# Four attention layers in turn, sliding and full: operand loads two quads ahead, layer norm by token tile, output weights in one load, and squares formed as they fall due

## The chip, the cores and the metric

The kernel runs on one core of one Trainium2 chip. The metric is the device time of one execution in microseconds (us), taken as the median of several runs. A core has a TensorE (PE) for matrix products, a VectorE (DVE), a ScalarE (ACT) and a GpSimd (POOL) for the rest, and a SyncE (SP), whose only work in this kernel is to issue DMA transfers, one after the other, from one queue.

## The reference

One sequence of S = 2048 tokens, width D = 512, H = 32 heads of Dh = 16, float32. Two kinds of attention alternate, each on the layer norm of the running sum. The A layers see a window of the last 256 tokens, the B layers all tokens, with no causal mask.

```python
def _A_ref(x, wqkv, wo):                       # layers 0 and 2
    qkv = (x @ wqkv).reshape(B, S, 3, H, Dh)   # transposed to q, k, v of (B, H, S, Dh)
    scores = jnp.einsum("bhqd,bhkd->bhqk", q, k) * (Dh ** -0.5)
    mask = (idx[:, None] - idx[None, :] >= 0) & (idx[:, None] - idx[None, :] < W)   # W = 256
    scores = jnp.where(mask[None, None], scores, -1e9)
    o = jnp.einsum("bhqk,bhkd->bhqd", _softmax(scores), v)
    return o.transpose(0, 2, 1, 3).reshape(B, S, D) @ wo

# _B_ref (layers 1 and 3): the same without the mask

x = A_x
x = x + _A_ref(_layernorm(x), A_wqkv, A_wo)
x = x + _B_ref(_layernorm(x), B_wqkv, B_wo)
x = x + _A_ref(_layernorm(x), A_wqkv, A_wo)
x = x + _B_ref(_layernorm(x), B_wqkv, B_wo)
```

## The kernel before

**Tiling.** The 2048 queries are four chunks c of 512, the 32 heads eight quads of four. A sliding layer goes through the chunks, in each through the eight quads, in each through three score steps; a step forms scores of two pairs of heads on PE (`s<-qt,kt`, L760), takes the exponential of each pair on ACT (`e<-s`, L764), cuts the window's edges on POOL (L832, L835) and adds to the sums with PE (L842). A full layer has sixteen steps a quad, each with two exponentials of 128 x 1024 (scores L756, sums L809). Layer 3 is cut once more by the four groups t of eight heads, so it has sixteen units (t, c) of two quads.

**Operands.** Products are kept exact by splitting numbers in two float16 parts. Queries and keys lie in DRAM as rows of such parts (`qs`, `kw` for sliding layers, `kf` for full ones). `load_win` (L786) and `load_full` (L773) bring the `qt` and `kt` of a quad; there are two `qt` buffers and three `kt` buffers, and `attention` (L1016) issues the loads of a quad one quad ahead. Weights are loaded raw (`load_w`, L314, tiles `wr`), split by ACT and DVE (`split`, L326) and stored to DRAM (`wd`); each use loads a megabyte from there. The raw and split weights use the four `vf` buffers, which in the full layers hold the values. The output weights (s = 3) are loaded as eight pieces of 16 partitions, since their rows have to lie in another order. Weights in use sit in two rings: ring 0 (`w`, two slots) and ring 1 (`vw`, three slots).

**Side work.** Between the score steps stand the projections of the next chunk or layer (`keys`, `queries`, `values`), the output product `wo` with the residual sum, and the layer norm of what comes out (`norm`). Each is a generator in a `Work`; a `Side` spreads a chunk's works over its steps, opens their weights ahead (`prefetch`, `may_open`), and `finish` runs what is left at the end of a chunk or unit. Between two layers lies a tail, in which the last chunk's output, norm and first projections run with no attention beside them.

**What sets the order.** PE's order, and in the full layers DVE's too, is the order in which this code issues it, by a clock of planned times (`clock[0]`): a work that waits gives a time before which it isn't taken up. On all other engines and in SP's queue a scheduler sets the order from priorities and its own estimates. Each engine, and SP's queue, then runs strictly in its order.

**Squares.** Softmax needs bounds: for every chunk the largest sum of squares of a key (`km`, L569) and each query's own (`m`, L595) are formed from the projected `sp` by POOL or DVE (`sq`), PE (`b<-sq,hsum`, L550, L553) and DVE. `keys` and `queries` put that on the list `pend` with a due time, 3.6 planned us later (4.6 in full layers), and `settle` does what is due. The keys of layers 1 and 3 share one maximum per head group over all chunks, and `key_shift` stores what follows from it; in layer 3 a work of its own, `shift3`, settles everything on the list and calls it.

**Layer norm.** `norm` has its passes over the four 128-token tiles of a chunk (three each, L449 and L455) issued by `turns` (L252), in sliding layers all at once; the transposes through the DMA (L477) follow.

A path for inputs outside of the bounds stands behind the kernel and does not run here.

Of the kernel before, what the change touches and what calls it, by code (L numbers as in the profile page):

```python
# [19 lines left out]
P = 128  # L20
# [170 lines left out]
def fast_path(ctx, tc, flag, a_x, a_wqkv, a_wo, b_wqkv, b_wo, out):  # L191
# [76 lines left out]
    ident = cp.tile([P, P], F32, name="ident")  # L268
# [45 lines left out]
    def load_w(ty, s):  # L314
        raw = wp.tile([P, NC, D], F32, name=f"wr{ty}_{s}", tag="vf", bufs=NQ)
        if s < 3:
            nc.sync.dma_start(raw, mats[ty, s].rearrange("(k p) f -> p k f", p=P))
        else:

            for u in range(2):  # L320
                for h in range(4):
                    nc.sync.dma_start(raw[32 * h + DH * u:32 * h + DH * u + DH],
                                      mats[ty, s].rearrange("(k u h d) f -> u h d k f", u=2, h=4, d=DH)[u, h])
        return raw

    def split(ty, s, raw):  # L326

        w = wp.tile([P, NC, 2, D], F16, name=f"w{ty}_{s}", tag="vf", bufs=NQ)
        for k in range(NC):
            nc.scalar.activation(w[:, k, 0], raw[:, k], AF.Copy, scale=WS)  # L330
            nc.vector.scalar_tensor_tensor(w[:, k, 1], raw[:, k], WS, w[:, k, 0], op0=ALU.mult, op1=ALU.subtract)
            yield
        nc.sync.dma_start(wd[ty, s], w)
        return w
# [150 lines left out]
    def project(l, s, c, act, ht=None):  # L485
# [3 lines left out]
        w = weights(ty, s, n, *((0, D, 0) if ht is None else (ht * P, (ht + 1) * P, l == 3 and not act)))  # L489
# [70 lines left out]
    def keys(l, c, act, ht=None, then=None):  # L560
        sqs = yield from project(l, 1, c, act, ht)
# [10 lines left out]
        pend.append((clock[0] + (4.6 if PH["full"] else 3.6), rest))  # L572

    def queries(l, c, act, ht=None):
        sqs = yield from project(l, 0, c, act, ht)
# [22 lines left out]
        pend.append((clock[0] + (4.6 if PH["full"] else 3.6), rest))  # L598
# [30 lines left out]
    def early_queries(l):  # L629

        PRE["q"] = pp.tile([P, 2, QC], F16, name=f"qt{l}_0_0", tag="qt", bufs=2)
# [39 lines left out]
    def wo(l, c, tail):  # L671
# [4 lines left out]
        for i in range(4):  # L676
# [9 lines left out]
            if i == 3 and not PH["full"]:  # L686
                yield from norm(l + 1, c, xs, tail)
# [22 lines left out]
    def epilogue(l, c, qd, a):  # L710
# [14 lines left out]
        def scaled():  # L725
            den = ot[:, :, DH]
            nc.vector.tensor_tensor(lmin, lmin, den, ALU.min)
            nc.vector.tensor_add(lsum, lsum, den)
# [5 lines left out]
            nc.vector.tensor_tensor(OT[t][:, :, u, :], ot[:, :, :DH], r[:, :, None].broadcast_to([P, QC // 32, DH]), ALU.mult)  # L734

# [37 lines left out]
    def load_full(l, c, qd):  # L773
# [12 lines left out]
    def load_win(l, c, qd):  # L786
        n = f"{l}_{c}_{qd}"
        kt = pp.tile([P, 2, S // 2], F16, name=f"kt{n}", tag="kt", bufs=3)
        qt = pp.tile([P, 2, QC], F16, name=f"qt{n}", tag="qt", bufs=2)
# [60 lines left out]
    class Work:  # L850
# [25 lines left out]
        def may_open(self):  # L876
# [7 lines left out]
        done = begun = open = going = False  # L884
# [4 lines left out]
        def advance(self):  # L889
# [18 lines left out]
            elif isinstance(c, tuple):  # L908
                self.ready = c[1]
                return 0.0  # L910
            return c

    class Side:
# [65 lines left out]
        def share(self):  # L979
# [3 lines left out]
            if pend and not PH["busy"] and clock[0] >= max(PH["free"], pend[0][0]):  # L983
# [32 lines left out]
    def attention(l, works):  # L1016
# [5 lines left out]
        for t in range(NHT if l == 3 else 1):  # L1022
            for c in range(NQ):
# [9 lines left out]
                ops = load(l, c, qds[0])  # L1033
                for qd in qds:
# [8 lines left out]
                    nxt = load(l, c, qd + 1) if qd + 1 in qds else None  # L1043
# [25 lines left out]
                    ops = nxt  # L1069
# [18 lines left out]
    def K3(c, ht, act=False):  # L1088
        return Work(later(keys, 3, c, act, ht, key_shift if c == NQ - 1 and ht == 0 else None), PK / 4, ("K3", c, ht), [("T", 3, c)], True, ring=not act)

    def Q3(c, ht, act=False, after=()):
        return Work(later(queries, 3, c, act, ht), PK / 4, ("Q3", c, ht), [("T", 3, c), *after], True, ring=not act)

    def K1(ht, act=False):
        return Work(later(keys, 1, NQ - 1, act, ht, key_shift), PK / 4, ("K1", ht), [("T", 1, NQ - 1), ("P", 1, 1)], True)

    def shift3(ht):
        def gen():
            settle()
            key_shift(3, ht)  # L1100
            yield -1e-6
        return Work(gen(), 0.0, ("S3", ht), [("K3", c, ht) for c in range(NQ)])
# [68 lines left out]
    run(vals)  # L1171
    all_of([NN(1), T(0, 1)])
# [45 lines left out]
    def side3(t, c):  # L1218
        a = [last_lower(3)] if (t, c) == (0, 0) else []
        a += [Q3(c + 1, t)] if c < 3 else []  # L1220
        if t < 3:
            a.append(K3(c, t + 1))
            if c == 3:
                a += [shift3(t + 1), Q3(0, t + 1)]
        if t < 2 and (t or c > 1):
            a.append(upper(3, 2 * t + c // 2, range(2 * (c % 2), 2 * (c % 2) + 2)))
        if (t, c) != (0, 0):
# [7 lines left out]
             2: [VV(3, 0, True, (0,)), OO(2, 3, True), VV(3, 1, True, (0,), late(3)), VV(3, 2, True, (0,), late(3)), VV(3, 0, True, (1,), late(3)), T(3, 3), K3(3, 0, True)]}  # L1235
# [54 lines left out]
```

## Time and profile before

| what | value |
|---|---|
| median of 3 runs | 2723.62 us (2723.14 to 2728.02) |
| profiled execution, its own time | 2721.88 us |
| its span | 2720.2 us |
| mean granted clock of TensorE | 0.988 |
| PE / ACT / DVE / POOL busy, share of the span | 91% / 87% / 41% / 19% |
| DMA | 360.80 MB in 341159 packets, 117800 of them under 512 B |
| start | 0 to 50 us |
| layer 0 (sliding), then its tail | 50 to 426, to 474 us |
| layer 1 (full) | 474 to 1430 us |
| layer 2 (sliding), then its tail | 1430 to 1703, to 1746 us |
| layer 3 (full), end | 1746 to 2703, to 2720 us |

The profile is of one execution. A row of a timeline has the start, the duration, the engine, the line of the code, the operation, out<-in with sizes, the count, and in brackets the idle time ahead of it on its engine with what ended it. SPq is SP's queue of DMA issues; a row there has the time of issuing, not of landing. A row of waits has the engine, its line and what it waited for, then the total in us, the number of times and the longest.

### The profile page before, as it was taken

What the parts mean: (1) busy time and instruction counts of PE and PEld (TensorE: products, weight loads), DVE (VectorE), ACT (ScalarE), POOL (GpSimd) and SP (SyncE); (2) the same over time, 40 slices, a digit from 0 to 9 for tenths busy, and PEclk for the clock granted to TensorE, in tenths of its full rate; (3) what the DMA queues carried; (4) which work ended last, traced back from release to release, by engine and by line L of the source; (5) the groups of instructions that cost most, each with busy time, mean ns of one, the idle gap of its engine ahead of it and who ended that gap; (6) DMA issues with size and microseconds to landing.
All of it is one profiled execution on the core that took longest, in us unless ns stands there. A gap on an engine that the chain in (4) does not pass through costs nothing.

```text
span 2720.2 us, 113346 instructions
## 1 busy us (share of the span) xinstructions
PE 2487.6 (91%) x51023; PEld 1095.7 (40%) x51023; DVE 1110.8 (41%) x2342; ACT 2363.1 (87%) x2671; POOL 526.7 (19%) x1080
## 2 busy tenths in 40 slices
PE   7888999999998999999998999899999999988997
PEld 3233444444443444444443333544444444433332
DVE  5574554223434334334326666323333323333333
ACT  4575664999999999999995777499999999999996
POOL 1455551001100100100105778000000000000000
PEclk9999999999999999999999999999999999999999
DMA  8888865222324225333426565623233333334332
GB/s 283 233 253 248 241 193 162 82 90 86 108 91 126 92 90 138 94 100 102 110 71 192 160 194 148 167 72 117 81 107 100 96 96 105 109 106 123 122 118 98
DMA packets 341159, 360.80 MB, mean 133 GB/s; under 512 B 117800, under 2 KB 256568, under 8 KB 334392
## 3 DMA queue, kind: packets, MB, share of 16 engines
q1 hardware_dynamic: 340664, 353.46, 43.7%
q8 instruction: 401, 6.57, 1.0%
q14 instruction: 94, 0.77, 0.1%
HBM read 240.65 MB, written 96.99 MB: 124 GB/s over the span
## 4 chain that ended last, share of the span: by engine, by line
ACT 55%; PE 23%; issue 11%; DVE 7%; DMA 3%; POOL 1%; SPq 0%; ACTq 0%; DVEq 0%; POOLq 0%
ACT e L764 55%; PE b L403 9%; PE acc L842 4%; PE s L760 2%; PE acc L809 2%; PE s L756 2%; PE bs L403 1%; PE b L400 1%; DVE xh L455 1%; DVE xh L449 1%; DMA kt<-kw 1%; DVE xn L449 0%; DVE ot L723 0%; DMA wr<-in_A_wo_dram 0%; DMA wv<-wd 0%
## 5 line engine op out<-in xcount | busy, mean ns | idle before, releaser
L764 ACT ACTIVATE e<-s 128x1024 f32<-128x1024 f32 (+2 forms) x2432 | 2240.7, 1056 | 149.9 <-PE s L760 101.0
L809 PE MATMUL acc<-e,vt 64*17 64x512 f32 x16384 | 1085.6, 590 | 1.0 <-issue 1.0
L756 PE MATMUL s<-qt,kt 64*32 64x512 f16 x16384 | 850.8, 381 | 121.4 <-ACT e L764 99.8
L756 PEld LDWEIGHTS <-kt 64*32 64x32 f16 x16384 | 407.0, 89 | 931.3 <-issue 852.0
L809 PEld LDWEIGHTS acc<-e,vt 64*17 64x17 f32 x16384 | 281.0, 92 | 61.8 <-issue 3.8
L835 POOL TENSOR_SCALAR_AFFINE_SELECT e<-e 128x256 f32<-128x256 f32 x512 | 224.9, 445 | 189.7 <-ACT e L764 188.5
L832 POOL TENSOR_SCALAR_AFFINE_SELECT e<-e 128x256 f32<-128x256 f32 x448 | 199.2, 450 | 94.4 <-ACT e L764 91.9
L842 PE MATMUL acc<-e,vt 128*17 128x384 f32 (+2 forms) x2816 | 201.8, 394 | 6.4 <-POOL e L832 6.2
L741 POOL TENSOR_TENSOR oh<-o,oh 128x512 f16<-128x512 f32 x31 | 36.1, 1163 | 702.0 <-DVE oh L740 676.0
L403 PE MATMUL b<-xc,w 128*128 128x512 f16 x660 | 161.7, 392 | 9.8 <-DVE km L569 5.5
L706 DVE SCALAR_TENSOR_TENSOR x<-b,x 128x512 f32<-128x512 f32 x122 | 83.9, 688 | 193.1 <-PE b L400 189.8
L760 PE MATMUL s<-qt,kt 64*128 64x384 f16 (+2 forms) x1408 | 121.3, 279 | 43.7 <-ACT e L764 20.4
L422 DVE TENSOR_SCALAR sa<-acc 128x512 f32<-128x512 f32 x64 | 44.2, 691 | 281.4 <-PE acc L809 281.4
L528 POOL TENSOR_TENSOR sq_h<-sp_h 128x512 bf16<-128x512 f16 x29 | 42.9, 1479 | 546.4 <-DVE sp_h L522 537.6
L528 POOL TENSOR_TENSOR sq<-sp 128x512 bf16<-128x512 f16 x32 | 46.2, 1443 | 519.7 <-DVE sp L522 475.2
L400 PE MATMUL b<-xc,w 64*32 64x512 f16 x3072 | 126.5, 376 | 2.7 <-DVE j L423 1.5
L400 PE MATMUL b<-xc,w_h 64*32 64x512 f16 x2784 | 111.0, 376 | 3.9 <-DVE km L569 3.9
L400 PE MATMUL b<-wo,oh 64*32 64x512 f16 x2592 | 109.1, 376 | 5.4 <-DVE x L706 3.0
L403 PEld LDWEIGHTS <-w 128*128 128x128 f16 x720 | 67.0, 100 | 116.3 <-issue 46.4
L422 DVE TENSOR_SCALAR vt<-b 128x256 f32<-128x256 f32 (+1 forms) x36 | 18.4, 512 | 232.9 <-PE b L400 232.9
L760 PEld LDWEIGHTS <-kt 64*128 64x128 f16 x1408 | 52.0, 95 | 140.9 <-issue 114.8
L422 DVE TENSOR_SCALAR j_h<-b 128x512 f32<-128x512 f32 x29 | 20.0, 689 | 206.6 <-PE b L400 206.6
(134 smaller groups left out, 1905.9 us busy)
## 6 DMA issues: line engine op xcount, KB each, us to landing
kt<-kf SPq DMA_DIRECT2D x128, 512.0 KB
qt<-qs SPq DMA_DIRECT2D x128, 256.0 KB
xd<-x SPq DMA_DIRECT2D x96, 256.0 KB
x<-xd SPq DMA_DIRECT2D x96, 256.0 KB
w<-wd SPq DMA_DIRECT2D x21, 1024.0 KB
kt<-kw SPq DMA_DIRECT2D x64, 256.0 KB
qs<-sp SPq DMA_DIRECT2D x48, 256.0 KB
wo<-wd SPq DMA_DIRECT2D x12, 1024.0 KB
```

The costliest lines, as they stand in the source:

```text
L400: nc.tensor.matmul(ps[g:g + 32, r], a[k, g:g + 32], b[k], start=(i == 0), stop=(i == len(pairs) - 1), skip_group_check=True)
L403: nc.tensor.matmul(ps, a, b, start=(i == 0), stop=(i == len(pairs) - 1))
L422: nc.vector.tensor_scalar(dst, ps[0], scale, None, op0=ALU.mult)
L528: nc.gpsimd.tensor_tensor(sq, sp[:, 0], sp[:, 0], ALU.mult)
L706: nc.vector.scalar_tensor_tensor(xs[i], p, 1 / WS, xs[i], op0=ALU.mult, op1=ALU.add)
L756: nc.tensor.matmul(ps[g:g + 32, h], kt[R * h:R * h + R, pr, kc + g:kc + g + 32], qt[R * h:R * h + R, pr], start=True, stop=True, skip_grou ...
L760: nc.tensor.matmul(ps[:, h, s0:s0 + wd_], kt[R * h:R * h + R, pr, kc:kc + P], qt[R * h:R * h + R, pr, qc:qc + wd_], start=True, stop=True)
L764: nc.scalar.activation(e[:, :, w0:w1], ps[:, :, w0:w1], AF.Exp, scale=SCALE)
L809: nc.tensor.matmul(acc[r][32 * h:32 * h + DH + 1, :], V[l, qd // 4, j // 8][k, j % 8, 4 * (qd % 4) + h, :], es_[h // 2][k, h % 2, :], star ...
L832: nc.gpsimd.affine_select(v, v, pattern=[[0, 2], [-1, P]], compare_op=ALU.is_gt, fill=0.0, base=0, channel_multiplier=1)
L835: nc.gpsimd.affine_select(v, v, pattern=[[0, 2], [1, P]], compare_op=ALU.is_ge, fill=0.0, base=0, channel_multiplier=-1)
L842: nc.tensor.matmul(a[32 * h:32 * h + DH + 1, q * P:(q + nb) * P], V[l, (4 * c + j) // 4][:, j % 4, 4 * qd + h, :], es_[h // 2][:, h % 2, s ...
```

## The change

Lines of the changed kernel are shifted by up to five from those of before.

- Sliding layers keep two quads' operands loaded ahead (`ahead`, with a third `qt` buffer), and the first quad of layer 0 is loaded at the end of the start.
- `turns` waits, in sliding layers, between an operation of the layer norm and the next, so that the passes of one token tile are issued at a time.
- The output weights come in one load of 128 partitions; their eight pieces are now made in the store to `wd`.
- A work `wo` declares its weights' slot free after its last product (`freed`), ahead of the norm that follows in it. In the tails ring 1 may be opened, and the key projections there use it.
- Squares are due after 1.2 planned us in the tails. `share` also waits for the planned DVE, `finish` also waits for what is under way while squares are pending. `shift3` is gone: `key_shift` is called with the last chunk's keys when their squares fall due.
- The memset of the sliding layers' values goes from POOL to DVE, and three small things change place (`lmin` and `lsum` in the epilogue, and the buffer of `ident`).

```diff
@@ turns (L252)
-        for us, f in ops:
+        for i, (us, f) in enumerate(ops):
             soon(chain, us, lambda f=f: one(f))
+            if PH["win"] and i < len(ops) - 1:
+                yield wait(us + 0.7)
@@ load_w (L314)
-        if s < 3:
-            nc.sync.dma_start(raw, mats[ty, s].rearrange("(k p) f -> p k f", p=P))
-        else:
-            for u in range(2):
-                for h in range(4):
-                    nc.sync.dma_start(raw[32 * h + DH * u:32 * h + DH * u + DH],
-                                      mats[ty, s].rearrange("(k u h d) f -> u h d k f", u=2, h=4, d=DH)[u, h])
+        nc.sync.dma_start(raw, mats[ty, s].rearrange("(k p) f -> p k f", p=P))
@@ split (L326)
-        nc.sync.dma_start(wd[ty, s], w)
+        if s < 3:
+            nc.sync.dma_start(wd[ty, s], w)
+        else:
+            for u in range(2):
+                for h in range(4):
+                    r, p = 32 * h + DH * u, P // 2 * u + DH * h
+                    nc.sync.dma_start(wd[ty, s][r:r + DH], w[p:p + DH])
@@ keys, queries
-    def keys(l, c, act, ht=None, then=None):
-        sqs = yield from project(l, 1, c, act, ht)
+    def keys(l, c, act, ht=None, then=None, ring=0):
+        sqs = yield from project(l, 1, c, act, ht, ring)
...
-        pend.append((clock[0] + (4.6 if PH["full"] else 3.6), rest))
+        pend.append((clock[0] + (4.6 if PH["full"] else 3.6 if PH["win"] else 1.2), rest))
@@ values (L651)
-            nc.gpsimd.memset(vt[:, :, :, DH:], 1.0)
+            nc.vector.memset(vt[:, :, :, DH:], 1.0)
@@ wo
             if i == 3 and not PH["full"]:
+                if not tail:
+                    yield "freed", clock[0]
                 yield from norm(l + 1, c, xs, tail)
@@ load_full, load_win, early_queries
-        qt = pp.tile([P, 2, QC], F16, name=f"qt{n}", tag="qt", bufs=2)
+        qt = pp.tile([P, 2, QC], F16, name=f"qt{n}", tag="qt", bufs=3)
@@ Work.may_open
-                    (len(wused[self.ring]) < RINGS[self.ring] or wused[self.ring][-RINGS[self.ring]].done) and (PH["full"] or not self.ring)
+                    (len(wused[self.ring]) < RINGS[self.ring] or wused[self.ring][-RINGS[self.ring]].done or wused[self.ring][-RINGS[self.ring]].freed) and not (PH["win"] and self.ring)
@@ Side.share, Side.finish
-            if pend and not PH["busy"] and clock[0] >= max(PH["free"], pend[0][0]):
+            if pend and not PH["busy"] and clock[0] >= max(PH["free"], pend[0][0], vt_[0] - 0.2):
...
-            while any(not stays(w) for w in self.q):
+            while any(not stays(w) for w in self.q) or PH["busy"] and pend:
@@ attention
-                ops = load(l, c, qds[0])
+                ahead = deque([PRE.pop("w", None) or load(l, c, qds[0])])
+                if win:
+                    ahead.append(load(l, c, 1))
...
-                    nxt = load(l, c, qd + 1) if qd + 1 in qds else None
+                    ops = ahead.popleft()
+                    if qd + 1 + win in qds:
+                        ahead.append(load(l, c, qd + 1 + win))
@@ K3, K1, side3, start, tails
-        return Work(later(keys, 3, c, act, ht, key_shift if c == NQ - 1 and ht == 0 else None), PK / 4, ("K3", c, ht), [("T", 3, c)], True, ring=not act)
+        ring = not act if ring is None else ring
+        return Work(later(keys, 3, c, act, ht, key_shift if c == NQ - 1 else None, ring), PK / 4, ("K3", c, ht), [("T", 3, c)], True, ring=ring)
...
-        return Work(later(keys, 1, NQ - 1, act, ht, key_shift), PK / 4, ("K1", ht), [("T", 1, NQ - 1), ("P", 1, 1)], True)
+        return Work(later(keys, 1, NQ - 1, act, ht, key_shift, act), PK / 4, ("K1", ht), [("T", 1, NQ - 1), ("P", 1, 1)], True, ring=act)
...
-    def shift3(ht):
-        def gen():
-            settle()
-            key_shift(3, ht)
...
+    PRE["w"] = load_win(0, 0, 0)
     all_of([NN(1), T(0, 1)])
...
-                a += [shift3(t + 1), Q3(0, t + 1)]
+                a.append(Q3(0, t + 1))
...
-             2: [..., T(3, 3), K3(3, 0, True)]}
+             2: [..., T(3, 3), K3(3, 0, True, True)]}
```

How the orders move is shown at three places. The first is SP's queue at the start of layer 0, before; `w_1_1` is a megabyte of key weights, `xc_1` the transposed norm of chunk 1, and `qt_0_0` the queries of chunk 0, quad 0:

```order
L597 DMA qs_0_97<-m_0_None 8x512 x4
L369 DMA w_1_1_556<-wd_1_106 128x4096
L477 DMA_TRANSPOSE xc_1_529<-xh_1_0_510 128x8x128
L791 DMA qt_0_0_535<-qs_0_97 128x2x512
L477 DMA_TRANSPOSE xc_1_529<-xh_1_1_515 128x8x128
```

And after:

```order
L599 DMA qs_0_97<-m_0_None 8x512 x4
L796 DMA kt_0_2_542<-kw_92 128x2x512
L795 DMA qt_0_0_477<-qs_0_97 128x2x512
L795 DMA qt_0_1_539<-qs_0_97 128x2x512
L795 DMA qt_0_2_543<-qs_0_97 128x2x512
L371 DMA w_1_1_560<-wd_1_106 128x4096
L479 DMA_TRANSPOSE xc_1_533<-xh_1_0_514 128x8x128
```

Three quads' queries now stand ahead of the weights and the transposes. The second place is SP's queue where the output weights `wr_3` of the A layers come in, in chunk 0 of layer 0, before:

```order
L369 DMA wv_1_0_0_915<-wd_2_107 128x4096
L322 DMA wr_3_917<-in_A_wo_dram 16x4x512 x8
L791 DMA qt_0_4_936<-qs_0_97 128x2x512
L792 DMA kt_0_4_935<-kw_92 128x2x512
L477 DMA_TRANSPOSE xc_2_957<-xh_2_0_792 128x8x128
```

After:

```order
L795 DMA qt_0_4_749<-qs_0_97 128x2x512
L796 DMA kt_0_4_748<-kw_92 128x2x512
...
L371 DMA wv_1_0_0_904<-wd_2_107 128x4096
L318 DMA wr_3_906<-in_A_wo_dram 128x4x512
L795 DMA qt_0_5_923<-qs_0_97 128x2x512
L796 DMA kt_0_5_922<-kw_92 128x2x512
```

Quad 4's operands stand ahead of the load, and the load is one row. The eight pieces are now stores (`wd_3<-w_3 16x4096 x8`), which stand right ahead of the raw weights of layer 1 and the first operands of chunk 1. The third place is DVE in chunk 1 of layer 0, before; `xn_3` and `xh_3` are the passes of chunk 3's norm, `km` the keys' maximum of chunk 2:

```order
L449 TENSOR_SCALAR xn_3_2_1691<-x_14_1497,mv_3_1657,y_3_1667 128x512
L734 TENSOR_TENSOR op_1_0_1754<-ot_1_0_1747,r_1_0_1751 128x16x16
L455 TENSOR_TENSOR xh_3_2_1692<-xn_3_2_1691,xh_3_2_1692 128x512
L449 TENSOR_SCALAR xn_3_3_1696<-x_15_1499,mv_3_1657,y_3_1667 128x512
L455 TENSOR_TENSOR xh_3_3_1697<-xn_3_3_1696,xh_3_3_1697 128x512
L569 TENSOR_REDUCE km_336<-b_1867 128x1
L516 SCALAR_TENSOR_TENSOR sp_0_2_0_1873<-b_1805,sp_0_2_0_1873 128x512
```

After:

```order
L451 TENSOR_SCALAR xn_3_0_1743<-x_12_1498,mv_3_1662,y_3_1672 128x512
L451 TENSOR_SCALAR xh_3_0_1744<-x_12_1498,mv_3_1662,y_3_1672 128x512
L451 TENSOR_SCALAR xh_3_1_1793<-x_13_1500,mv_3_1662,y_3_1672 128x512
L457 TENSOR_TENSOR xh_3_0_1744<-xn_3_0_1743,xh_3_0_1744 128x512
L451 TENSOR_SCALAR xh_3_2_1853<-x_14_1502,mv_3_1662,y_3_1672 128x512
L571 TENSOR_REDUCE km_336<-b_1865 128x1
L518 SCALAR_TENSOR_TENSOR sp_0_2_0_1871<-b_1800,sp_0_2_0_1871 128x512
```

The maximum stood behind all twelve passes and now stands behind five. In the same way the split of layer 1's output weights (`w_3`), which stood behind the norm that follows chunk 0's output, now stands ahead of it. On PE, the score steps of layer 2 with no side product behind them are 34 of 96 (26 before), since products of `keys` collect at the ends of its chunks; in layer 3 the last step of two units (t = 1, chunks 1 and 3) now has 96 side products behind it, all of `values`, and in layer 1 one step has 48, where 32 was the most.

More of the change, by code (lines that the diff above doesn't have):

```diff
@@ L483, in transpose, with project @@
             transposed(l, c, i, xh)
-    def project(l, s, c, act, ht=None):
+    def project(l, s, c, act, ht=None, ring=0):
         ty, n = l % 2, f"{l}_{s}_{c}" + ("" if ht is None else f"_h{ht}")
-        w = weights(ty, s, n, *((0, D, 0) if ht is None else (ht * P, (ht + 1) * P, l == 3 and not act)))
+        w = weights(ty, s, n, *((0, D, 0) if ht is None else (ht * P, (ht + 1) * P, ring)))
         yield wait(8)
@@ L571, in rest, with queries @@
                     then(l, ht)
[L572 to L575 removed]
+        pend.append((clock[0] + (4.6 if PH["full"] else 3.6 if PH["win"] else 1.2), rest))
+    def queries(l, c, act, ht=None, ring=0):
+        sqs = yield from project(l, 0, c, act, ht, ring)
         def rest():
@@ L597, in rest @@
                 nc.sync.dma_start(rows(qs[l % 2, c])[8 * t:8 * t + 8, 3, :], m[32 * t:32 * t + 8, :])
-        pend.append((clock[0] + (4.6 if PH["full"] else 3.6), rest))
+        pend.append((clock[0] + (4.6 if PH["full"] else 3.6 if PH["win"] else 1.2), rest))
     def settle(all_=True):
```

22 lines of the change are left out of this document (10 added, 12 removed).

## The prediction

> **What bounds the kernel now.** The time is spread over stages with different limits, so the view that comes first is the table of stretches: layer 0 fills 50 to 426 us, a tail to 474, layer 1 to 1430, layer 2 to 1703, a tail to 1746, layer 3 to 2703. Its columns are the stretch, its length, the busy time of each engine with its count, the granted TensorE clock, the DMA share and GB/s.
>
> ```profile
> core 0: us, PE busy (x) PEld busy (x) DVE busy (x) ACT busy (x) POOL busy (x), PEclk, DMA share, GB/s
> 0.00:50.00 50.00, 37.19 (x168) 17.75 (x168) 33.02 (x84) 21.43 (x37) 2.66 (x15) 1.00 0.80 284
> 50.00:215.00 165.00, 131.91 (x1088) 47.94 (x1088) 102.57 (x243) 100.39 (x141) 79.01 (x189) 0.92 0.91 254
> 215.00:426.00 211.00, 203.65 (x1860) 84.86 (x1860) 102.30 (x239) 136.77 (x168) 117.02 (x296) 0.99 0.74 216
> ...
> 1430.00:1703.00 273.00, 250.22 (x2552) 94.87 (x2551) 173.66 (x407) 191.88 (x226) 200.15 (x481) 0.98 0.61 174
> ...
> 1746.00:2703.00 957.00, 874.05 (x21806) 387.98 (x21797) 310.83 (x582) 943.99 (x1024) 57.23 (x42) 1.00 0.34 104
> ```
>
> Layer 3 (layer 1 reads alike) is a chain of exponentials: ACT is busy 944 of 957 us, so little of PE's work there is worth anything. The sliding layers are PE's: in layer 0 PE idles 165.00 - 131.91 = 33 us of the first stretch and 7 of the second, in layer 2 23 us. The gain of an edit in a sliding layer is an idle time of PE that goes. So the next view is what PE waited for in layer 0 (total, times, longest), and then in layer 2:
>
> ```profile
> PE s L760 <- DMA kt<-kw: 9.0, 2, 8.2
> PE s L760 <- ACT e L764: 8.6, 14, 1.9
> PE acc L842 <- POOL e L832: 5.6, 2, 5.1
> PE b L403 <- DVE km L569: 5.5, 1, 5.5
> PE s L760 <- DMA qt<-qs: 4.2, 1, 4.2
> PE b L553 <- DVE sp L516: 3.9, 1, 3.9
> PE b L403 <- DMA w<-wd: 3.4, 1, 3.4
> ```
>
> ```profile
> PE s L760 <- ACT e L764: 11.8, 20, 1.1
> PE s L760 <- DMA qt<-qs: 7.4, 3, 3.6
> PE s L760 <- DMA kt<-kw: 1.6, 1, 1.6
> ```
>
> A few large waits make the idle time, most of them for operands that a DMA brings late. After such a wait the next matmuls run slowly: 16 took 5.31 us behind the wait for w (3.43 us in brackets), 3.56 us in the chain of work that ended last, where nothing was waited for. A restart costs 1.75 us, then, or less.
>
> ```profile
> 386.76 5.31 PE L403 MATMUL b<-xc,w 128*128 128x512 f16 x16 [3.43 <-DMA w<-wd]
> ...
> 393.61 3.56 PE b L403 x16
> ```
>
> **The change part by part, layer 0.** The worst wait is that for kt at 104 us. The timeline of SP's queue, and of PE, has:
>
> ```profile
> 86.97 8.41 SPq L322 DMA_DIRECT2D wr<-in_A_wo_dram  x8
> 96.00 0.39 SPq L791 DMA_DIRECT2D qt<-qs  x1
> 96.94 0.39 SPq L792 DMA_DIRECT2D kt<-kw  x1
> ...
> 104.19 0.82 PE L760 MATMUL s<-qt,kt 64*128 64x384 f16 x4 [8.21 <-DMA kt<-kw]
> 105.93 2.71 PE L403 MATMUL b<-xc,w 128*128 128x512 f16 x8
> ```
>
> The eight loads of the output weights hold the queue for 8.41 us, and the operands of the next quad stand behind them. After the change one load stands there (the seven others at 8.41 / 8 = 1.05 us each are 7.4 us of queue gone), and the quad's operands stand ahead of it, a quad earlier. I take the 8.2 us, and the restart: 2.71 us against half of 3.56, 0.9 us. **9.1 us**; below that 7.4, above it nothing more, as the wait can't give more than itself. The other kt wait of layer 0 (9.0 - 8.2 = **0.8**) goes too.
>
> The first qt (4.2 us) is issued late, behind a megabyte of weights that the order now puts after it:
>
> ```profile
> 45.15 0.35 SPq L369 DMA_DIRECT2D w<-wd  x1
> ...
> 50.51 0.51 SPq L791 DMA_DIRECT2D qt<-qs  x1
> ```
>
> It moves up by some 5 us, more than the wait; three loads now share the place, one ahead of it (0.4 us): **3.8**. The weights and transposes that it passes come 2 us later; they feed side work some steps on, so nothing for that.
>
> The wait for km comes from DVE's order: the squares' maximum stands behind the whole norm of a chunk.
>
> ```profile
> 157.38 0.54 DVE L449 TENSOR_SCALAR xn<-x,mv,y 128x512 f32<-128x512 f32 x1
> ...
> 165.56 0.68 DVE L569 TENSOR_REDUCE km<-b 128x1 f32<-128x512 f32 x1
> 166.29 3.23 PE L403 MATMUL b<-xc,w 128*128 128x512 f16 x8 [5.55 <-DVE km L569]
> ```
>
> In the new order five of the twelve passes of the norm stand ahead of it, so of the 8.2 us from 157.38 to 165.56 some 4 to 5 go, and with a short wait most of the restart (3.23 - 1.78 = 1.4): 4.0 + 1.0 = **5.0** (0 if DVE comes to it late by other work, 7 at most). The sp wait (3.9) keeps its passes in front, the norm's first two tiles and an epilogue: **0.4**. The wait for selects (5.1) is POOL's:
>
> ```profile
> 210.96 0.32 POOL L647 MEMSET vt<- 128x128 f32 x1 [10.59 <-DVE w L331]
> ```
>
> A memset of a layer-1 buffer waits 10.59 us on POOL for the weight split that last reads that buffer, and the selects queue behind it. It stays on POOL and keeps its place, but the split now stands on DVE ahead of the norm, not behind it: **4.0** (0 to 5.1). The memsets of the window's values, of the same 0.32 us on POOL, move to DVE: nothing, as DVE is free in two fifths of the stretch (eight of them, 2.6 us, if it were not).
>
> These are 9.1 + 0.8 + 3.8 + 5.0 + 0.4 + 4.0 = 23.1 us, all in the first stretch. Its DMA share is 0.91, and the bytes stay the same: 0.09 x 165 = 15 us is what the queues leave. I take **12** of the 23. The w wait at 387 us is the slot of a weight ring, which now opens before the norm ends: 3.4 + 1.75 less a rest, **4**. Layer 0: 16.
>
> On this cap a rule speaks the other way: the Trainium skill, page DMA: Bandwidth & Descriptors, section Specifications, gives about 358 GB/s per core to memory and wants transfers of 512 B or more. The trace moves 254 GB/s at share 0.91, so by that figure the estimate is 165 x 254 / 358 = 117 us of traffic, and the whole 23 could be had; by the share only 15. The trace of before can't tell which is right there.
>
> **Layer 2.** The qt and kt waits, 7.4 + 1.6 = 9.0, go with the loads two ahead, and one restart:
>
> ```profile
> 1479.91 5.21 PE L403 MATMUL b<-xc,w 128*128 128x512 f16 x16 [0.78 <-DMA qs<-m_None]
> ```
>
> 5.21 - 3.56 = 1.65. Against it, the new order bunches projection work at the ends of the chunks and leaves 34 score steps with nothing between them, where 26 were. Such a step waits for ACT: 11.8 / 26 = 0.45 us each, so eight more cost 3.6 (nothing if the load ahead shortens them, 8 x 1.1 = 8.8 at the longest wait). 9.0 + 1.65 - 3.6 = **7.0**.
>
> **Tails.** In the first and the second tail PE waited for
>
> ```profile
> PE b L403 <- DMA wv<-wd: 2.2, 1, 2.2
> PE bs L403 <- DMA w_h<-wd: 1.1, 1, 1.1
> ...
> PE b L403 <- DMA wv<-wd: 1.7, 1, 1.7
> PE b L403 <- DMA w_h<-wd: 1.3, 1, 1.3
> ```
>
> The K1 and K3 weights go to another ring and wait for no slot of wv: 3.3 + 3.0 = **6.3**. Squares due earlier fill waits that PE hardly has there: nothing.
>
> **Full layers.** What ACT waited for in layer 3, and one of three alike (1942, 2191 and 2429 us):
>
> ```profile
> ACT e L764 <- PE s L756: 11.7, 11, 2.1
> ...
> 1942.25 37.98 ACT L764 ACTIVATE e<-s 128x1024 f32<-128x1024 f32 x41 [1.84 <-PE s L756]
> ```
>
> At these three, PE settled all squares at once and went through POOL and DVE for it; formed as they fall due they cost ACT nothing: 5.5 gained. In their place two units of layer 3 end in 96 bunched matmuls of the values each, and layer 1 has a step with 48 of the keys. By the groups of lines in layer 3,
>
> ```profile
> L400 PE MATMUL b<-xc,w_h 64*32 64x512 f16 x2592 | 103.3, 376 | 3.9 <-DVE km L569 3.9
> ...
> L400 PE MATMUL b<-wv,xc 64*32 64x256 f16 x1344 | 29.1, 274 | 0.4 <-issue 0.4
> ```
>
> 96 take 29.1 / 1344 x 96 = 2.1 us of PE and the 48 take 103.3 / 2592 x 48 = 1.9. What ACT loses is 0 if enough scores stand ready and all of it if none do; I take 1.84, as at a settle, for each of the two, 3.7, and half a settle for the 48, since steps with 32 are there today: 0.9. Layer 3 **1.8**, layer 1 **-0.9**.
>
> **New waits.** Loads two ahead can themselves hold the queue, and eight stores replace one:
>
> ```profile
> SPq L791 <- PE s L760: 20.0, 10, 5.8
> ```
>
> That is what SP waited for a free operand slot in layer 0. I allow three new waits of PE at 1.6, the smaller kt wait of layer 2: **+4.9** (0 to 10). Sum: 16 + 7.0 + 6.3 + 1.8 - 0.9 - 4.9 = 25.3. The profiled execution took 2721.88 us (span 2720.2), 1.7 under the median of 2723.62: 2721.9 - 25.3 + 1.7 = **2698**.
>
> **The rivals.**
> - DMA is the bound of the first stretch: operands issued earlier only push the weights later. For it: share 0.91, and that the kt at 96.94 took 7 us to land. Against it: it stood behind eight loads of 128 KB in 2 KB rows, which had just been issued. The stretch then gives nothing, and 25.3 - 12 = 13 us remain: 2711.
> - The change does not do what it says: DVE comes to km and to the split when it did before, since the passes are due by their data and not by their row, and the stalls of the sliding layers go to the next operand. Left are the settles, the tails and half of layer 2: 1.8 + 6.3 + 3.5 - 0.9 = 10.7 us, less the 4.9: 2718.
> - The cap of 15 us is no cap: the share of busy time counts requests that wait for each other too. In the first row of the table the queues moved 284 GB/s at a share of 0.80, or 355 at a full one, by which the first stretch's traffic takes 165 x 254 / 355 = 118 us. Against it: the rows there are longer ones, of inputs and weights. The whole 23 us come then, and with no new waits the time is 2721.9 - 25.3 - 11 - 4.9 + 1.7 = 2682.
> - Slower: SP's queue is in order, and a load two quads ahead waits until the quad before has given its slot back. One ahead it did so ten times in layer 0, 2.0 us each; now every one of the 60 or so loads of two layers may, and behind it stand stores of keys and queries, transposes and weights that side work needs. Where PE waits next for one of them, each hold costs 2 us. The gains of 30 us are used up at 15 such holds on PE's path, and 20 make 40 us: 2733. Against it: the third qt buffer keeps the lag at one quad, so that a hold has a quad's time to be hidden ((426 - 50) / 32 = 12 us in layer 0), and the weights have rings of their own.
>
> **How the numbers follow.** The forecast, 2698, with its own range of 2688 to 2708, holds 0.55; no cap 0.10; DMA bound 0.15; not as it says 0.12; slower 0.08. The range leaves out the slower case, about half of the one that does nothing (the half past its 2718), and what lies more than 6 us below the case without a cap: 2676 to 2719. Measurements of this kernel tell 0.2%, 5.4 us, from no change, so faster means below 2718: 0.55 + 0.10 + 0.15 and a sixth of the case that does nothing, 0.82; the rest of that case, 0.10, lies within; slower 0.08.
>
> **What would show it.** In layer 0's waits the rows of kt, qt and km shrink to under 2 us each; the 10.59 on POOL is a small number; the stretch from 50 us to the end of the first two chunks is 10 to 15 us shorter at a DMA share above 0.95, where a share of 0.91 and the old length would speak for the first rival. Layer 2's qt row goes and its ACT row grows to about 15. In layer 3 the three gaps of 1.84 are gone and two others appear. What makes it wrong: SP held by L791 for much more than 20 us in a layer, or PE waiting for weights and transposes where it waited for operands.

## The result, and the profile after

The changed kernel takes 2700.8 us (median of 4 runs, 2699.32 to 2702.92) against 2724.3 us of the kernel before: 23.5 us less, a ratio of 0.9906 with a 95% interval of 0.9894 to 0.9918. Forecast were 2698 us, in a range of 2676 to 2719. The profiled execution of the changed kernel took 2702.92 us with a span of 2701.1; that of before lay 2.4 us under its median and this one 2.1 over, so that the two profiles show 19 us of the 23.5.

The stages are cut at the first exponential of each, as the timeline of ACT has them. "Again" is a second profile of the unaltered changed kernel (first experiment), which tells how much of a difference is scatter.

| stage, us | before | after | again |
|---|---|---|---|
| start | 54.2 | 50.7 | 50.3 |
| layer 0, chunks 0 / 1 / 2 / 3 | 81.9 / 101.5 / 93.8 / 93.6 | 79.9 / 94.6 / 93.4 / 88.3 | 81.1 / 93.4 / 93.1 / 88.3 |
| tail | 49.3 | 45.2 | 45.2 |
| layer 1 | 954.3 | 960.6 | 961.1 |
| layer 2, chunk 0 / the others | 72.5 / 198.9 | 66.7 / 196.8 | 66.7 / 193.2 |
| tail | 46.1 | 47.8 | 49.2 |
| layer 3, first to last exponential | 953.1 | 958.1 | 957.2 |
| end | 21.1 | 19.1 | 18.8 |

The sliding layers and the start give 26 us (18.1 in layer 0 with the start, 7.9 in layer 2), the first tail 4. The full layers take 11 back, which nobody who looks at the total alone would see. What PE waited for in layer 0 (47 to 408 us) of the changed kernel, in total, times and longest:

```profile
PE s L764 <- ACT e L768: 7.5, 14, 1.0
PE b L555 <- DVE sp L518: 5.0, 1, 5.0
PE b L405 <- DMA xc<-xh: 4.1, 1, 4.1
PE b L405 <- DVE km L571: 4.1, 1, 4.1
PE b L555 <- ACT sq L528: 3.3, 1, 3.3
PE s L764 <- DMA kt<-kw: 0.7, 1, 0.7
PE acc L846 <- POOL e L836: 0.5, 1, 0.5
```

The waits for operands (9.0 and 4.2 us before) are gone but for 0.7 us, those for the weights (3.4) and for POOL (5.1) altogether. Two are new: one for the transposes `xc` and one for a square that ACT forms. In layer 2 (1412 to 1677 us) and in the second tail:

```profile
PE s L764 <- ACT e L768: 12.1, 23, 1.1
PE b L405 <- DMA xc<-xh: 2.9, 1, 2.9
```

```profile
PE s L760 <- DMA kt<-mk: 1.8, 2, 1.6
PE b L405 <- DMA wv<-wd: 1.6, 1, 1.6
PE bs L405 <- DMA wv<-wd: 0.3, 1, 0.3
```

Layer 2 has no wait for qt or kt any more. In the tail the wait for `w_h` is gone, that for `wv` is not. The stretches that answer to those of before show nearly the same work in less time (the counts differ by up to 4%, since the cuts don't fall at quite the same places):

```profile
47.00:208.00 161.00, 139.07 (x1127) 51.95 (x1125) 102.11 (x249) 100.93 (x143) 84.50 (x189) 0.95 0.92 271
208.00:408.00 200.00, 196.14 (x1848) 81.86 (x1840) 105.07 (x249) 136.99 (x168) 119.52 (x293) 1.00 0.77 225
...
1412.00:1677.00 265.00, 247.96 (x2521) 94.33 (x2515) 170.77 (x408) 191.95 (x226) 199.43 (x473) 0.99 0.61 176
...
1724.00:2684.00 960.00, 876.01 (x21806) 386.70 (x21806) 309.89 (x582) 945.76 (x1024) 57.53 (x42) 1.00 0.34 104
```

In the first row the DMA share is 0.92 as it was (0.91), but the queues move 271 GB/s where they moved 254. In the last one the stretch is 3 us longer at the same work: ACT, the bound there, waits more.

### The profile page after: what moved, and what is told of

The parts are those of the page before. It is cut to its first block, busy times and chain, and to the rows that moved or that the text cites. A ratio compares the mean times of both kernels' runs of the same rounds, so it can differ in the third digit from the quotient of the medians.

```text
span 2701.1 us, 113344 instructions
## 1 busy us (share of the span) xinstructions
PE 2488.5 (92%) x51023; PEld 1094.3 (41%) x51023; DVE 1103.9 (41%) x2350; ACT 2365.4 (88%) x2671; POOL 535.2 (20%) x1072
## 4 chain that ended last, share of the span: by engine, by line
ACT 56%; PE 25%; issue 12%; DVE 4%; DMA 2%; POOL 1%; SPq 0%; ACTq 0%; DVEq 0%; POOLq 0%
ACT e L768 55%; PE b L405 11%; PE acc L846 4%; PE acc L813 3%; PE s L764 2%; PE s L760 2%; PE bs L405 2%; PE b L402 1%; POOL e L839 1%; POOL e L836 1%; DMA xc<-xh 0%; DMA wv<-wd 0%; DMA kw<-zeros 0%; DMA x<-in_A_x_dram 0%; DMA qs<-ones 0%
## 5 line engine op out<-in xcount | busy, mean ns | idle before, releaser
L839 POOL TENSOR_SCALAR_AFFINE_SELECT e<-e 128x256 f32<-128x256 f32 x512 | 234.0, 465 | 159.7 <-ACT e L768 159.1
L836 POOL TENSOR_SCALAR_AFFINE_SELECT e<-e 128x256 f32<-128x256 f32 x448 | 201.6, 456 | 104.6 <-ACT e L768 100.8
L424 DVE TENSOR_SCALAR j<-b 128x512 f32<-128x512 f32 x32 | 22.0, 688 | 203.7 <-PE b L402 203.7
```

What stands on the lines that cost most here:

```text
L424: nc.vector.tensor_scalar(dst, ps[0], scale, None, op0=ALU.mult)
L836: nc.gpsimd.affine_select(v, v, pattern=[[0, 2], [-1, P]], compare_op=ALU.is_gt, fill=0.0, base=0, channel_multiplier=1)
L839: nc.gpsimd.affine_select(v, v, pattern=[[0, 2], [1, P]], compare_op=ALU.is_ge, fill=0.0, base=0, channel_multiplier=-1)
```

## The experiments

The spread alone is an edit of the kernel before, all others are of the changed kernel, and all compute the whole reference. Medians are of 4 to 11 runs each; the kernel before was at 2724.4 to 2726.5 us beside them. Two medians that are 3 us apart are not told from equal: the changed kernel's own runs go from 2698.6 to 2709.5 us.

**The changed kernel again**, with no edit.

> The changed kernel once more, unaltered. In its first profile layer 1 took 6.3 us and layer 3 about 5 us more (first to last exponential) than in the kernel before, though three waits of 1.84 us are gone. Theory: that is in the order, and this profile shows it again: layer 1 at 954 to 957 us, layer 3 at 957 to 959, with five waits of ACT of about 1.2 us at the same five exponentials of layer 3. Rival: it is the scatter of single executions, and the layers lie within 2 us of before's 950.1 and 953.1 now. Time 2700.8, within 2.

Measured: 2701.3 us (2698.6 to 2709.5). Layer 3 took 957.2 us and shows the same five waits at the same exponentials, layer 1 took 956.2 us from its first to its last exponential (950.1 before, 955.7 in the change's first profile). So the longer full layers lie in the order of the program. PE's timeline at one of the five waits, in the changed kernel's first profile, DVE's rows in the same place, and a row of ACT's behind them:

```profile
2008.34 0.38 PE L552 MATMUL b<-sq_h,hsum 64*32 64x512 bf16 x2
2010.22 0.39 PE L552 MATMUL b<-sq_h,hsum 64*32 64x512 bf16 x2 [1.50 <-DVE m L587]
2010.22 0.60 PE L760 MATMUL s<-qt,kt 64*32 64x512 f16 x8
...
2008.76 0.68 DVE L586 TENSOR_SCALAR m<-b 32x512 f16<-32x512 f32 x1 [2.52 <-PE b L552]
2009.48 0.68 DVE L587 SCALAR_TENSOR_TENSOR m<-b,m 32x512 f16<-32x512 f32 x1
...
2010.94 1.02 ACT L768 ACTIVATE e<-s 128x1024 f32<-128x1024 f32 x1 [1.21 <-PE s L760]
```

Two squares stand behind one another. A full layer has one PSUM tile for such products, so the second pair waits 1.5 us until DVE has read the first (`m`, two passes), the scores behind it wait too, and ACT stands idle for 1.21 us.

**One due square at a time.**

```diff
             if pend and not PH["busy"] and clock[0] >= max(PH["free"], pend[0][0], vt_[0] - 0.2):
-                settle(False)
+                pend.pop(0)[1]()
```

> In the full layers one due square is formed at a time, not all that are due. Theory: with the added wait for the planned DVE, the squares of a query and of a key group fall due together in five places of layer 3; the second's matmuls wait 1.5 us for DVE to read the one bank, ACT loses 1.2 to 1.4 us each. Then the five waits go, 6 to 7 us: 2694 to 2695 us, layer 3 at 951 to 952 us. Rival: the waits come from DVE being late for each square, and move on to other steps: 2700 to 2701 us.

Measured: 2692.6 us (2689.0 to 2699.8), a ratio of 0.9887 (0.9869 to 0.9906) to the kernel before: 8 us better than the change. Layer 3 took 948.3 us. What ACT waited for in layer 3, of the changed kernel (1724 to 2684 us) and then of this one:

```profile
ACT e L768 <- PE s L760: 12.4, 13, 1.7
```

```profile
ACT e L768 <- PE s L760: 4.6, 6, 1.7
```

The five waits (1.21 us each, 6 us) are gone, and 8 of 12 us of waiting in all.

**Without the wait for the planned DVE** in `share` (`max(PH["free"], pend[0][0])`, as before).

> The changed kernel without the wait for the planned DVE ahead of squares in the full layers (the rest of the change stays). Theory: without it the squares are formed singly as they fall due and no pair meets at the bank: the five waits of layer 3 go, 2694 to 2696 us. Rival: the wait kept PE from standing behind a busy DVE; without it PE waits for DVE in other steps as long or longer: 2700 to 2704 us.

Measured: 2697.9 us (2696.8 to 2700.2). Layer 3 took 949.2 us, with none of the five waits, so it is this condition that made two squares fall due together. But the end after the last exponential took 23.8 us (19.1 with the change, 21.1 before): products of the output that the change had run beside attention were left over. The theory holds for the waits; by the medians the time gained 3 us and not 6, which is within the scatter.

**The squares of the full layers as before**: `shift3` back, no wait for DVE, the old `finish`.

> The squares of the full layers as before (the separate work that settles all, no wait for the planned DVE, the old end of a unit); all else of the change stays. Theory: the three waits of 1.84 us come back (+5.5), the five of 1.2 to 1.4 and the two bunches of 96 go (-7 to -9): 2697 to 2700 us. Rival, my prediction's sum: the part gains 1.8 us in layer 3, so that undoing it gives 2702 to 2703 us.

Measured: 2699.3 us (2697.0 to 2701.1), as the theory has it: layer 3 took 954.5 us with the three waits of 1.8 us back, and the five gone. The part of the change that was to help the full layers is worth nothing (the medians say -1.5 us, which the runs can't tell from none). Layer 1, from its first to its last exponential, stays at 954.8 us against 950.1 before, so most of its 5 us are not from this part.

**Sliding operands one quad ahead.**

```diff
-                if win:
-                    ahead.append(load(l, c, 1))
...
-                    if qd + 1 + win in qds:
-                        ahead.append(load(l, c, qd + 1 + win))
+                    if qd + 1 in qds:
+                        ahead.append(load(l, c, qd + 1))
```

> The changed kernel with the operands of sliding layers one quad ahead again (third buffer for queries and the early load of the very first quad stay). Theory: the loads two ahead took away the waits of PE for qt and kt, 9.0 us in layer 2 with a restart of 1.7, and in layer 0 those that the single load of the output weights didn't take, 1 to 9 us: 2710 to 2718 us. Rival: the third query buffer and the single load alone took them, the second quad ahead is spare: 2701 to 2704 us.

Measured: 2703.1 us (2699.9 to 2706.1), the rival's time. Layer 2's first chunk, where I had laid the gain, took 66.5 us, as with the change (66.7). In layer 0 PE waited 5.1 us for kt, in three waits of 2.7 at most, and 1.3 for qt, where the change has 0.7 and none.

**The output weights in eight loads**, one store each (both edits of `load_w` and `split` undone).

> The changed kernel with the output weights of both types in eight loads again, one store each. Theory: with operands two quads ahead the wait of 8.2 us at 104 us is covered by a quad's 12 us though the queue is held 8 us twice, so the single load is worth 0 to 3 us: 2700 to 2704 us. Rival, the step of my prediction that gave the single load its 7.4 us: the queue held for 8 us makes PE wait for other rows behind it, 7 to 9 us: 2708 to 2710 us.

Measured: 2699.7 us (2696.3 to 2700.7). The single load alone is worth nothing here; PE waited once for kt in layer 0, 3.3 us.

**Both undone together.**

> The changed kernel with sliding operands one quad ahead and the output weights in eight loads, both undone together. Undone singly they cost 2 us and nothing, and the wait of 8.2 us for kt at 104 us came back in neither. Theory: each covers that wait by itself, and without both it is back, with its restart, in the first chunk of layer 0: 2709 to 2713 us, a wait for kt of 7 to 8 us in layer 0. Rival: a third part, the spread of the norm that moved the transposes away from the loads, took it: 2701 to 2705 us and no such wait.

Measured: 2720.3 us (2717.5 to 2726.0): more than the theory's 2709 to 2713, and 19.5 us over the change where the two alone cost 2.3 and -1.1. Two rows of PE's timeline in layer 0, and SP's queue ahead of the first of these waits:

```profile
106.51 0.82 PE L764 MATMUL s<-qt,kt 64*128 64x384 f16 x4 [8.67 <-DMA kt<-kw]
...
210.83 1.03 PE L764 MATMUL s<-qt,kt 64*128 64x128 f16 x8 [8.78 <-DMA kt<-kw]
```

```profile
90.45 7.58 SPq L324 DMA_DIRECT2D wr<-in_A_wo_dram  x8
98.45 0.39 SPq L795 DMA_DIRECT2D qt<-qs  x1
99.43 0.39 SPq L796 DMA_DIRECT2D kt<-kw  x1
```

The wait at the A weights is that of before; a second of the same size stands at the B weights, where before had 0.80 (it comes with the spread of the norm, see below). Either edit covers most of both waits, so each looks worthless when it alone is undone.

**The norm's passes at once** (the waits in `turns`, the spread for short, undone).

> The changed kernel with the passes of a chunk's layer norm issued all at once again. Theory: the spread moved the split of layer 1's output weights ahead of a norm on DVE, which freed POOL, and km ahead of seven passes; undone, the wait of POOL of 10 us and PE's behind it (5.1) come back and km's wait grows by 1.4 to 5 us: 2706 to 2710 us. Rival: km gained only 1.4 us by it and POOL's wait went for another reason (the slot declared free early, the single load): 2700 to 2703 us.

Measured: 2721.1 us (2718.5 to 2725.2), 20 us over the change and far past either expectation. Chunk 3 of layer 0 took 96.3 us (88.3), chunk 0 of layer 2 73.1 (66.7), chunk 1 of layer 0 98.5 (94.6). What PE waited for in layer 0 (47 to 426 us), the first rows, and in layer 2 (1420 to 1700 us):

```profile
PE s L762 <- ACT e L766: 9.5, 17, 1.0
PE b L403 <- DMA w<-wd: 6.0, 1, 6.0
PE b L403 <- DVE km L569: 5.3, 1, 5.3
```

```profile
PE s L762 <- ACT e L766: 11.6, 22, 1.1
PE s L762 <- DMA kt<-kw: 4.2, 1, 4.2
PE b L403 <- DMA xc<-xh: 4.1, 2, 2.8
```

The wait for km is 1.2 us longer than with the change, a little less than the theory's least case. POOL's memset waits 3.99 us, not 10, and PE doesn't wait behind it. The rest are waits for transfers: weights (`wv` too, 4.1 us in layer 0), keys, transposes. SP's queue at the wait for w, which ends at 380.79 us:

```profile
370.57 1.24 SPq L477 DMA_TRANSPOSE xc<-xh  x1
371.92 0.53 SPq L369 DMA_DIRECT2D w<-wd  x1
372.54 7.99 SPq L477 DMA_TRANSPOSE xc<-xh  x2
380.62 0.53 SPq L793 DMA_DIRECT2D qt<-qs  x1
```

The last two transposes hold the queue for 8 us, with the next quad's operands behind them. That hold alone is not what costs: in the next run two transposes hold the queue for 8.19 us at the same place (368.32 us), right behind a load of w, and PE waits for no weights there.

**The passes at once, but the norm's end planned later.**

```diff
         for us, f in ops:
             soon(chain, us, lambda f=f: one(f))
+        if PH["win"] and len(ops) > 1:
+            yield wait(sum(us + 0.7 for us, _ in ops[:-1]))
```

> The changed kernel with the passes of a chunk's norm issued all at once, as before, but with the norm's end, its transposes and what follows planned later by the same 10.6 planned us that the spread takes. Undoing the spread as a whole cost 20 us, 8 of them in chunk 3 of layer 0 and 6 in chunk 0 of layer 2. Theory: what counts is not where the passes stand on DVE (km stands behind eight of twelve passes without the spread, five with it) but that the transposes and the products of the normed chunk, and the operand loads around them in SP's queue, are placed later, when their data is there: 2699 to 2704 us. Rival: the order of the passes on DVE is what counts: 2717 to 2723 us.

Measured: 2697.2 us (2694.5 to 2698.0), as good as the change or better. It isn't the order of the passes that counts: PE waits for km as long as with the passes at once (5.5 us against 5.3). The planned end is: transposes and products are placed 10.6 planned us later. The wait for w in layer 0 is gone, and so are those for kt and xc in layer 2 (1408 to 1675 us):

```profile
PE s L764 <- ACT e L768: 13.1, 25, 1.1
PE acc L846 <- POOL e L836: 0.7, 2, 0.5
PE b L405 <- DMA qs<-m_None: 0.4, 1, 0.4
```

**The spread alone**, on the kernel before.

> The kernel before with the spread of the norm's passes as its only edit. Theory: the spread is most of the change: 2703 to 2708 us, with layer 2's first chunk at 66 to 67 us and layer 0's last at 88 to 92 us. Rival: it works only together with the earlier slots and the loads ahead, and alone it moves waits: 2715 to 2724 us.

Measured: 2724.7 us (2721.9 to 2731.6), a ratio of 0.9999 (0.9989 to 1.0009). What PE waited for in layer 0 (50 to 426 us):

```profile
PE s L762 <- DMA kt<-kw: 20.4, 3, 9.9
PE s L762 <- ACT e L766: 8.7, 16, 1.0
PE b L405 <- DVE km L571: 5.8, 1, 5.8
PE s L762 <- DMA qt<-qs: 4.0, 1, 4.0
```

The wait for w is gone, and chunk 0 of layer 2 gains 1.6 us. But the waits for kt, 9.0 before, are 20.4. At the A weights it is 9.94 us (8.21 before), at the B weights 8.67 (0.80). At the B weights SP's queue now has two transposes (5.57 us), the eight loads (4.56) and four stores (3.85) in a row ahead of kt; before, the four transposes there were through 4.7 us ahead of the loads. With nothing to bring operands sooner, the spread loses there what it gains elsewhere.

**Weight slots freed late**, ring 1 shut outside of the full layers (the key projections of the tails back in ring 0).

> The changed kernel with weight slots freed only at the end of a work and ring 1 shut outside of the full layers, as before. Theory: the wait for w in chunk 3 of layer 0 comes back (3.4 and a restart of 1.75, that chunk 5 us longer), and in the tails the waits for w_h (1.1 and 1.3) and for wv in the first (2.2): 2708 to 2711 us. Rival: these waits went since the loads stand elsewhere in the queue: 2701 to 2703 us.

Measured: 2703.4 us (2702.1 to 2706.3), between the two. Chunk 3 of layer 0 is 3.6 us longer than in the second profile of the change and the first tail 2.9 us, but layer 1's first chunk is 2.1 us shorter: the slots gain 6 us by these two profiles and a part is given back there. In the first tail the waits for `w_h` (1.05) and `wv` (1.58) are back, as the theory has it; the wait for w in chunk 3 is not. By the medians the whole is 2 to 3 us, within the scatter.

**Both edits that helped**: the norm's end planned later, and one due square at a time.

> Both edits that helped, together: the norm's passes issued at once with its end planned later, and one due square at a time in the full layers. Theory: they act in different layers, so their gains against the changed kernel (4.1 and 8.7 us by the medians) add up: 2687 to 2691 us, layer 3 at 948 to 949 us. Rival: the gain of the first was scatter (the two medians of the changed kernel differ by 0.5, its runs by 10 us): 2691 to 2695 us.

Measured: 2690.8 us (2688.0 to 2692.7), a ratio of 0.9870 (0.9853 to 0.9886) to the kernel before. Layer 3 took 946.6 us. That it beats the change is clear; that it beats one due square alone (2692.6) is not.

## Why the prediction was right, and where its steps were wrong

The time was right to 3 us, in part by luck. Several of the terms were not right, and the reasons for some that were right in size fell.

- **The operands in layer 0** (9.1 + 0.8 of kt). The wait went, as said. The step took it as the work of the single load and of the loads ahead together; each does most of it alone (3.3 us of kt are left with the eight loads, 5.1 with one quad ahead), and without both it is 8.67 + 8.78 = 17.5 us in the layer and not 9.
- **The start** (3.8). The first exponential came 3.5 us sooner. The clause "they feed side work some steps on, so nothing for that" was wrong. With attention sooner and the transposes later, PE stood before the latter for 4.11 us, and restarted at 4.44 us for 12 products, which take 2.76 elsewhere; it is a row of the changed kernel's timeline:

```profile
60.88 4.44 PE L405 MATMUL b<-xc,w 128*128 128x512 f16 x12 [4.11 <-DMA xc<-xh]
```

- **km** (5.0). Its wait shrank from 5.5 to 4.1 us and the restart stayed. The five passes ahead of km took 2.65 us where all twelve, with what stood between them, took 8.18, as DVE's timeline of the changed kernel has it, followed by PE's row:

```profile
155.76 0.59 DVE L451 TENSOR_SCALAR xn<-x,mv,y 128x512 f32<-128x512 f32 x1
...
158.41 0.68 DVE L571 TENSOR_REDUCE km<-b 128x1 f32<-128x512 f32 x1
159.14 3.57 PE L405 MATMUL b<-xc,w 128*128 128x512 f16 x8 [4.05 <-DVE km L571]
```

  But PE's wait began at 159.14 - 4.05 = 155.09, 0.7 us before the norm did, where it had begun 3.4 us into it (160.74 against 157.38). The new order saves 5.5 us ahead of km, but PE now comes there 4 us earlier against the norm, so its wait shrank by 1.5 only. The step had taken the moment of PE's arrival as fixed.
- **POOL's memset** (4.0 of 5.1). Right in size: its 10.59 us are 0.99, and PE's 5.1 are gone. The reason, the split ahead of the norm on DVE, does not carry it: with the norm's passes at once it waits 3.99 us, and 10.40 with the norm spread but both operand edits undone. With the norm spread and one of these two edits kept it is 3.55 or 2.35.

```profile
202.51 0.33 POOL L649 MEMSET vt<- 128x128 f32 x1 [0.99 <-DVE w L326]
```

- **The cap of 15 us** by the DMA share. The first stretch (start, chunks 0 and 1) gave 12.4 us, and I had taken 12, but not for that reason: the share stayed at 0.92 (the sign was to be above 0.95) while GB/s rose to 271. What stands between it and the whole 23 are waits of PE: 4.1 for xc and 1.7 for the restart behind it, 3.3 for the square, 1.1 more for sp, and the 3.6 that km did not give. Only that for xc is for a transfer, so the trace does not show full queues as the bound. The figure of the Trainium skill, page DMA: Bandwidth & Descriptors, section Specifications, about 358 GB/s per core to memory, which left room for the 23, is neither confirmed nor contradicted: the most that a stretch moves here is 284 GB/s.
- **The w wait** (4). Chunk 3 of layer 0 gave 5.3 us. What takes the wait away is the later planned end of the norm: without it a wait for w of 6.0 us and 8 us of the chunk come back, and the spread alone, with no slot freed early, has no wait for w. Without the free slot 3.6 us of the chunk come back, but no wait for w; where they go is not traced.
- **Layer 2** (7.0). It gave 7.9 and 11.5 us in the two profiles, but "go with the loads two ahead" was wrong: with one ahead the waits stay away, and with the norm's end planned early one for kt (4.2 us) comes back beside two for xc. The spread alone leaves 5.3 us of waits for qt, so another part of the change is needed too; the third `qt` buffer, which stays in the runs with one quad ahead, is a candidate that was not tried by itself. Eight more bare steps were to cost 3.6; the wait for ACT grew from 11.8 to 12.1 us. Of the gain in its last chunk, 12 products of `w_h` (2.76 us) went over into the tail.
- **Tails** (6.3). The first gave 4.1, the second cost 1.7 and 3.1. The wait for `wv` was not for a slot that the other weights held: on SP the load of the later `wv` still waits until PE has used up the one before, and PE then waits for it to land.
- **Layer 3** (1.8 gained). This is the step that failed: "formed as they fall due they cost ACT nothing". The three settles are gone, but five pairs of squares meet at one PSUM tile and cost ACT 1.21 us each, and the layer took 5.0 and 4.1 us longer. The two bunches of 96 products, put at 1.84 us each, cost ACT 0.44 and 1.53 (PE's wait of 0.90 for the next qt is in the latter). Together that is 2.5 us more than the settles gave; the rest is not traced. One due square at a time brought the layer to 948.3 us, 4.8 under before and near the 5.5 that the step had promised.
- **Layer 1** (0.9 lost). It lost 6. One wait of 1.8 us is of the kind of layer 3's: an output product stands behind a square that DVE still reads. ACT loses 1.57 us by it, and does not in the two runs without the wait for the planned DVE.

```profile
774.27 0.63 PE L402 MATMUL b<-wo,oh 64*32 64x512 f16 x16 [1.82 <-DVE m_None L587]
```

About 2 us in its first chunk come with the slots (it is 237.5 us without them, 239.6 to 240.1 with them). The rest, some 2 us, I haven't traced.

So the sum came near by errors that cancel in part: the full layers cost 9 us (with the end) instead of giving 0.9, and the second tail cost where it was to give 3.0; against that, the new waits for which I had put 4.9 were already within what the sliding layers gave, and these gave 3 us more than their terms. By the two profiles the gain is 19 us, 6 short of the 25.3. That the medians lie within 3 us of the forecast is scatter in my favour, and luck.

Of the rivals, the slow one (SP held by loads two ahead) did not occur: SP waited for a slot on those lines 12.1 us in layer 0, in 9 waits, where it had been 20.0 in 10:

```profile
SPq L795 <- PE s L764: 12.1, 9, 4.2
```

The rival with the DMA as the bound of the first stretch is out with its 12.4 us, and the one without a cap (2682) did not come either.

What stays open: whether the later planned end of the norm acts through PE's order or through SP's queue, since both move with it; no run moved one without the other.

## What to carry to other kernels

Undo the parts of a change singly and together: two parts that cover the same waits looked worthless one by one and were worth 20 us as a pair, and a third part worth 20 us in the whole was worth nothing alone. In a program whose order is written ahead, when a result is *planned* to be ready decides what stands in front of what, and a plan that was too early cost 20 us here, where one 10.6 us later cost nothing. When small pieces of work are allowed to fall due, look for the buffer that two of them share: formed as a pair, they stalled PE for 1.5 us and ACT, the bound, for 1.21 behind it, five times in a layer.

## What the runs showed that I had not expected

The DMA share did not tell what was left of the queues: the first stretch moved 254 GB/s at 0.91 and then 271 GB/s at 0.92. And the issue of a transposing DMA held SP's queue for several us at times. All of the kernel before (durations min/median/max in ns), and the four of chunk 3 in layer 0 with the norm's passes at once:

```profile
L477 SPq DMA_TRANSPOSE xc<-xh x60: 1231/1336/5483, 49.0 to 1730.6; - x60
```

```profile
L477 SPq DMA_TRANSPOSE xc<-xh x4: 1244/1593/5968, 367.1 to 374.6; - x4
```

Most take 1.3 us. The longest of those four, 5.97 us, follows within 3 us of a megabyte of weights, and so do the other long ones of 4 us and more in both profiles but one. Ten of the sixty took over 2.5 us before, three with the change. That the weights in flight are the cause was not tried by itself.
